# Angles of the trigonometric tables as 16-bit fixed point, and no arithmetic on GpSimd, in a fused linear attention and FFT gate kernel

## The chip, the cores and the metric

The kernel runs on one core of one Trainium2 chip. The core has TensorE (matmuls), VectorE, ScalarE and GpSimd (arithmetic on tiles in on-chip memory) and SyncE (here only for issuing the stores). Each works through its own list of instructions in order and waits for the others by semaphores. The metric is the time of one execution in microseconds of the device. Before the change it is 284.3 us, the median of three runs (283.73 to 285.67).

## What is computed

The reference takes q, k and v (8 batches, 8 heads, 576 positions, 64 features) and does two things in a row. First a linear attention: with `theta = pi/2 * pos / 576`, q and k are passed through relu and doubled into a cosine and a sine half; then

```
kv  = einsum('bhsf,bhsd->bhfd', k_p, v)
num = einsum('bhsf,bhfd->bhsd', q_p, kv)
den = einsum('bhsf,bhf->bhs', q_p, sum(k_p over s))
att = num / (den + 1e-6)
```

The heads are put side by side into x (8 x 576 x 512). Then a gate with a long convolution:

```
x1, x2, x3 = split(x @ w_proj)                     # 512 x 1536
conv = irfft(rfft(x2) * rfft(filter_fft))          # over the 576 positions
out  = (x1 * conv * x3) @ w_out                    # 512 x 512
```

## The kernel before

The 576 positions are held as 96 partitions times 6. A batch goes through these steps, each a function in the code: `emit_phi` (VectorE: relu and the multiplication by cosine, sine or tangent columns, giving the tiles `qp` and `kp`; for q one relu over everything and six multiplications by `tcol`), `emit_va` (ScalarE copies v), `emit_kv` (TensorE), `emit_qt` (TensorE transposes `qp`, VectorE and ScalarE each copy half of the result into `qpt`), `emit_num` (TensorE, then VectorE divides: tile `att`), `emit_fx` (TensorE, a first small transform that also sorts positions; ScalarE copies to `fx`), `emit_x2` (TensorE: the x2 part of the projection, tile `x2f`), `emit_dft` (TensorE with the tables `tre` and `tim`, then VectorE multiplies by the filter's transform `h3`), `emit_gate` (TensorE: x1 and x3, 64 matmuls of 128x288 per batch in four column blocks; ScalarE copies x1 to `x1s`, VectorE multiplies it with x3 into `g`), `emit_inv` (TensorE with the tables `ire` and `iim`), `emit_out` (TensorE, ScalarE, store).

All matmul results go through one ring of four PSUM units (`unit`, line 62), shared by all steps. A step that asks for a fifth unit waits until the first one of the ring has been read. In `emit_gate` every column block takes two units, one that `x1s` frees and one that `g` frees.

The inputs are loaded by GpSimd's queue, with a conversion from 4 to 2 bytes an element, into a ring of four `raw` tiles. Batch 2's q, k and v and all later ones have to wait until an older tile has been read.

The tables are made by the kernel itself at its start, between the steps of batches 0 and 1. There are three sets, each a sine and a cosine table: the forward table (`tre`, `tim`, 96x288, `emit_fwd_tables`), the filter's table (`hs_`, `hc`, 96x864, `emit_h_tables`) and the inverse table (`ire`, `iim`, 96x864, `emit_inv_turns` and `emit_inv_tables`). Each is made in the same way. Index tiles from GpSimd (`fr_i`, `sr_i`, integers) times a factor give the angle in turns, as a float (`tn_fwd`, `tn_h`, `tn_inv`). [...] `sin_cos` (line 288) then has ScalarE take the sine, the absolute value, and a sine shifted by a quarter turn for the cosine (lines 290 to 292).

`emit_h` transforms the filter. The two halves of the filter (`filt16`, 96x1536 each) are added and subtracted into `feo`, on GpSimd (line 421), and TensorE multiplies them with the filter's tables. One row of the inverse table is made apart (`t0`, `t1`, lines 381 to 388).

The order on each engine comes from a scheduler, which takes the instructions by the order of the calls at the end of the program and by its own estimate of when each is ready. `behind(...)` holds an instruction back until a named earlier one has been issued: `feo` is held behind the second GpSimd operation of the inverse angles (the mark "turns"). The calls at the start run from batch 0's attention through `emit_rows`, `emit_inv_turns`, the four blocks of `emit_gate(0, c)`, `emit_fwd_tables`, `emit_x2(0)`, `emit_phi(1, "q")`, `emit_qt(1, .)`, `emit_h_tables`, `emit_phi(1, "k")`, `emit_kv(1)`, `emit_h`, `emit_num(1, .)` and `emit_dft(0)` to `emit_inv_tables` and batch 2. From batch 1 on a loop repeats the same steps without any tables.

Of the kernel before, what the change touches and what calls it, by code (L numbers as in the profile page):

```python
# [13 lines left out]
I32 = mybir.dt.int32  # L14
# [3 lines left out]
def kernel(  # L18
# [51 lines left out]
    half_pi = consts.tile([128, 1], FP32, tag="half_pi", name="half_pi")  # L70
    wr_col = consts.tile([128, 1], FP32, tag="wr_col", name="wr_col")
# [17 lines left out]
    def tsc(out, in0, s1, op0, s2=None, op1=None):  # L89
        if op1 is None:  # L90
            nc.vector.tensor_scalar(out=out, in0=in0, scalar1=s1, scalar2=None, op0=op0)
        else:
            nc.vector.tensor_scalar(out=out, in0=in0, scalar1=s1, scalar2=s2, op0=op0, op1=op1)  # L93
# [178 lines left out]
    def turns_off(nr, turns, ncol, pool=False):  # L272

        a_ = setupp.tile([NP, NCOL], FP32, tag="tg_a", bufs=2, name="tg_a")
        a = a_[0:nr, 0:ncol]
        if pool:
            nc.gpsimd.tensor_scalar(
                out=a, in0=turns, scalar1=RC, scalar2=-RC, op0=AL.add, op1=AL.add
            )
            mark["turns", 0] = nc.gpsimd.tensor_tensor(out=a, in0=a, in1=turns, op=AL.subtract)  # L280
        else:
            nc.vector.tensor_scalar(out=a, in0=turns, scalar1=RC, scalar2=None, op0=AL.add)
            nc.vector.scalar_tensor_tensor(
                out=a, in0=a, scalar=-RC, in1=turns, op0=AL.add, op1=AL.subtract
            )
        return a

    def sin_cos(nr, a, sin_dst, cos_dst):

        nc.scalar.activation(out=sin_dst, in_=a, func=AF.Sin, scale=TWO_PI)  # L290
# [5 lines left out]
    def trig(nr, turns, sin_dst, cos_dst, ncol):  # L296
        sin_cos(nr, turns_off(nr, turns, ncol), sin_dst, cos_dst)
# [22 lines left out]
    def emit_fwd_tables():  # L320
# [18 lines left out]
        tsc(q4, half, 0.25, AL.mult)  # L339
# [5 lines left out]
        trig(NP, tnf, tim.rearrange("p a b -> p (a b)"), tre.rearrange("p a b -> p (a b)"), HS)  # L345
# [17 lines left out]
    def emit_inv_turns():  # L363
        fc = cc["fc"]
        sr_i = cc["sr_i"]
        fcs = small("fcs", 3)
        tsc(fcs, fc, 1.0 / 1152.0, AL.mult)
        tn = setupp.tile([NP, NCOL], FP32, tag="tn_inv", name="tn_inv")
        for bl in range(3):
            nc.scalar.activation(  # L370
                out=tn[:, ds(bl * HS, HS)], in_=sr_i, func=AF.Copy, scale=fcs[0:NP, bl : bl + 1]
            )
        cc["inv_a"] = turns_off(NP, tn, NCOL, True)

    def emit_inv_tables():
        sr_i = cc["sr_i"]
        sin_cos(
            NP, cc["inv_a"], iim.rearrange("p a b -> p (a b)"), ire.rearrange("p a b -> p (a b)")
        )

        t0 = setupp.tile([1, HS], FP32, tag="t0", name="t0")
        tsc(t0, sr_i[0:1], 0.25, AL.mult)
        t1 = setupp.tile([1, HS], FP32, tag="t1", name="t1")
        tsc(t1, t0, RC, AL.add)
        nc.vector.scalar_tensor_tensor(
            out=t1, in0=t1, scalar=-RC, in1=t0, op0=AL.add, op1=AL.subtract
        )
        nc.scalar.activation(out=iim[0:1, 0], in_=t1, func=AF.Sin, scale=TWO_PI)

    def emit_h_tables():  # L390
# [9 lines left out]
        tn = setupp.tile([NP, NCOL], FP32, tag="tn_big", name="tn_h")  # L400
        for j in range(3):
            tsc(tn[:, ds(j * HS, HS)], frf, s3[0:NP, j : j + 1], AL.mult, 1.0 / S, AL.mult)
        trig(NP, tn, hs_.rearrange("p a b -> p (a b)"), hc.rearrange("p a b -> p (a b)"), NCOL)
# [12 lines left out]
    def emit_h():  # L416
        hc, hs_, hb, alt = cc["hc"], cc["hs"], cc["hb"], cc["alt"]
        fa = filt16.rearrange("p x (j n) -> p x j n", j=3)
        for x, op in ((0, AL.add), (1, AL.subtract)):
            with behind("turns", 0):  # L420
                nc.gpsimd.tensor_tensor(
# [31 lines left out]
    def emit_phi(b, nm, h0=0, nh=NH):  # L453
# [11 lines left out]
        for j in range(NJ):  # L465
            for cs, col in ((0, ccol), (1, scol)) if nm == "k" else ((1, tcol),):
                tsc(
# [372 lines left out]
```

## Time and profile before

| | |
|---|---|
| median of three runs | 284.3 us (283.73 to 285.67) |
| the profiled execution | 285.12 us |
| its span on the core | 283.3 us |
| TensorE busy (matmuls) | 250.7 us, 88% |
| VectorE busy | 218.8 us, 77% |
| ScalarE busy | 197.6 us, 70% |
| GpSimd busy | 38.8 us, 14% |
| mean granted TensorE clock | 0.973 of full |

The span is the time from the first to the last instruction on the core; the execution's time is 1.8 us longer. Busy time counts no waiting. In the chain that ended last, followed back from the last store, TensorE has 73% of the span, VectorE 14% and ScalarE 7%. The list of waits puts down each idle stretch of an engine to the instruction that came last before it ended; where several had to come, the named one need not be the one that was late for a reason of its own. The page's strip of 40 slices shows TensorE's share and its granted clock over time: TensorE is at 90% or more in nearly all slices behind the first third, and the granted clock is below 0.9 in three of the slices between 35 and 71 us.

### The profile page before, as it was taken

Reading aid. Unit: us, or ns where it says so; the run is one execution under the profiler, and the core shown is the slowest. Engines: PE = TensorE matmul, PEld = TensorE weight load, DVE = VectorE, ACT = ScalarE, POOL = GpSimd, SP = SyncE. Lnnn points to the kernel's source line nnn. Section 1 sums busy time; section 2 is a strip of 40 time slices with the busy share of each in tenths; the row PEclk is TensorE's granted clock in tenths of the full one; section 3 lists DMA queues with packets and bytes.
Section 4 is the critical chain, followed back from the end, with each engine's and each line's share of the span. In section 5 each row is a group of like instructions: output and inputs, shape, how many; then the busy total and the mean of one; then the engine's idle time right before and its main releaser. Section 6 shows DMA issues by size and latency. Waiting matters only on the chain.

```text
span 283.3 us, 6056 instructions
## 1 busy us (share of the span) xinstructions
PE 250.7 (88%) x2393; PEld 176.5 (62%) x2393; DVE 218.8 (77%) x666; ACT 197.6 (70%) x274; POOL 38.8 (14%) x51
## 2 busy tenths in 40 slices
PE   0387719998899999999999999999999999999991
PEld 0265516755676867686768676867687768755740
DVE  7789999698999768986799579965997269606650
ACT  2366236997948796869676976798679867758252
POOL 8443950130010111011100010010000000000000
PEclk9999957997999999999999999999999999999998
DMA  5999974698624069506960697065000500050405
GB/s 79 184 206 207 204 105 67 86 126 125 86 24 62 8 83 253 78 2 84 240 98 1 87 193 142 0 86 169 1 2 0 147 22 2 0 168 26 126 20 167
DMA packets 26989, 26.67 MB, mean 94 GB/s; under 512 B 1680, under 2 KB 22160, under 8 KB 26960
## 3 DMA queue, kind: packets, MB, share of 16 engines
q0 software_dynamic: 21200, 16.84, 41.3%
q1 hardware_dynamic: 5760, 9.44, 10.8%
q8 instruction: 18, 0.29, 0.4%
q14 instruction: 11, 0.09, 0.1%
HBM read 33.69 MB, written 9.44 MB: 152 GB/s over the span
## 4 chain that ended last, share of the span: by engine, by line
PE 73%; DVE 14%; ACT 7%; DMA 2%; issue 1%; POOL 0%; POOLq 0%
PE x L623 21%; PE x L586 14%; PE out L670 12%; PE inv L649 8%; PE qt L497 5%; DVE qp L93 5%; PE fx L549 4%; PE kv L484 4%; ACT x2f L591 4%; PE num L523 3%; DMA vraw<-in_v_dram 2%; PE dft L600 2%; DVE kp L93 2%; DVE att L533 1%; ACT va L122 1%
## 5 line engine op out<-in xcount | busy, mean ns | idle before, releaser
L623 PE MATMUL x<-fx,wp 128*128 128x288 f16 x512 | 69.9, 292 | 8.5 <-DVE tim L358 7.4
L623 PEld LDWEIGHTS <-wp 128*128 128x128 f16 x512 | 51.0, 100 | 22.3 <-DVE tim L358 7.7
L586 PE MATMUL x<-wp,fx 128*96 128x512 f16 x192 | 44.9, 380 | 0.0
L591 ACT ACTIVATE x2f<-x 96x1024 f16<-96x1024 f32 x24 | 24.5, 1019 | 25.7 <-PE x L586 25.7
L553 ACT CAST fx<-fx 128x960 f16<-128x960 f32 x32 | 30.7, 961 | 15.6 <-PE fx L549 15.6
L670 PE MATMUL out<-wo,y 128*128 128x512 f16 x160 | 37.8, 379 | 0.3
L122 ACT COPY va<-vraw 96x768 f16<-96x768 f16 x32 | 25.6, 846 | 8.9 <-DMA vraw<-in_v_dram 8.9
L586 PEld LDWEIGHTS <-fx 128*96 128x96 f16 x192 | 22.2, 123 | 14.3
L631 DVE TENSOR_TENSOR g<-x,x1s 128x288 f16<-128x288 f32 x64 | 27.2, 449 | 4.3 <-PE x L623 4.3
L533 DVE TENSOR_TENSOR att<-num,rcp 128x640 f16<-128x640 f32 x32 | 26.3, 821 | 0.3
L504 DVE COPY qpt<-qt 128x600 f16<-128x600 f16 x30 | 14.0, 468 | 15.8 <-PE qt L497 15.1
L670 PEld LDWEIGHTS <-y 128*128 128x128 f16 x160 | 15.1, 97 | 16.5 <-DVE y L656 1.2
L602 ACT CAST xf<-dft 96x1024 f16<-96x1024 f32 x24 | 23.5, 1009 | 1.9 <-PE dft L600 1.3
L605 DVE TENSOR_TENSOR m<-xf,h 96x1024 f16<-96x1024 f16 x24 | 16.3, 679 | 10.9 <-ACT xf L602 10.7
L674 ACT ACTIVATE os<-out 128x1024 f32<-128x1024 f32 (+1 forms) x24 | 21.4, 904 | 4.5 <-PE out L670 2.3
L484 PE MATMUL kv<-va,kp 96*128 96x65 f16 x384 | 15.4, 197 | 10.0 <-ACT va L122 8.4
L629 ACT CAST x1s<-x 128x576 f16<-128x576 f32 x32 | 20.4, 639 | 5.5 <-PE x L623 4.7
L497 PEld LDWEIGHTS <-qp 96*128 96x128 f16 x384 | 20.6, 102 | 5.4 <-issue 1.0
L93 DVE TENSOR_SCALAR qp<-qraw,tcol 96x512 f16<-96x512 f16 (+1 forms) x54 | 23.4, 493 | 0.0
L497 PE MATMUL qt<-perm,qp 96*128 96x96 f16 x384 | 22.2, 213 | 0.6 <-ACT fx L553 0.4
L649 PEld LDWEIGHTS <-yf 96*128 96x128 f16 x192 | 18.5, 98 | 5.1 <-DVE yf L609 0.7
L484 PEld LDWEIGHTS <-kp 96*128 96x128 f16 x384 | 14.3, 100 | 11.4 <-DVE kp L93 8.9
(172 smaller groups left out, 400.2 us busy)
## 6 DMA issues: line engine op xcount, KB each, us to landing
out_dram<-os SPq DMA_DIRECT2D x24, 192.0 KB, 2.7
qraw<-in_q_dram POOLq DMA_DIRECT2D x7, 576.0 KB, 7.4
kraw<-in_k_dram POOLq DMA_DIRECT2D x7, 576.0 KB, 7.6
vraw<-in_v_dram POOLq DMA_DIRECT2D x7, 576.0 KB, 6.2
out_dram<-os SPq DMA_DIRECT2D x24, 128.0 KB, 2.5
wp<-in_moe_w_proj_dram POOLq DMA_DIRECT2D x3, 512.0 KB, 11.9
out_dram<-os SPq DMA_DIRECT2D x24, 64.0 KB, 2.4
kraw<-in_k_dram POOLq DMA_DIRECT2D x2, 288.0 KB, 6.2
```

The source lines that it names most:

```text
L93: nc.vector.tensor_scalar(out=out, in0=in0, scalar1=s1, scalar2=s2, op0=op0, op1=op1)
L122: nc.scalar.copy(out=va_buf[b % 2][:, hs, :, 0:D], in_=raw_t[(b, "v")][:, hs].rearrange("p h (j d) -> p h j d", j=NJ),)
L484: nc.tensor.matmul(u[:, h // 4, ds((h % 4) * 65, 65)], kp[:, j, h].rearrange("p a b -> p (a b)"), va[:, h, j, 0:65], start=(j == 0), stop= ...
L497: nc.tensor.transpose(u[:, hh, ds(j * NP, NP)], qp[:, j, 2 * hp + hh].rearrange("p a b -> p (a b)"), perm,)
L533: mark["att", b, hp] = nc.vector.tensor_tensor(out=att[:, :, ds(hp * 128, 128)].rearrange("p t (h d) -> p h t d", h=2), in0=nv[:, :, :, 0: ...
L553: nc.scalar.copy(out=fx[:, c, :, 0:40].rearrange("p g (u o) -> p u g o", u=2), in_=u[:, :, 0:480].rearrange("p u (g o) -> p u g o", o=20),)
L586: nc.tensor.matmul(u[0:NP, comp], fx[:, c, ds(comp * 6 + 2 * bl, 2)].rearrange("p a b -> p (a b)"), wp16[:, c, ds(DM, DM)], start=(c == 0) ...
L591: mark["x2f", b, bl] = nc.scalar.mul(out=x2f[:, bl], in_=u[0:NP], mul=X2SC)
L623: nc.tensor.matmul(u[:, hf, 0:HS], wp16[:, i, ds(w * DM + c * 128, 128)], fx[:, i, ds(12 + 6 * hf, 6)].rearrange("p a b -> p (a b)"), star ...
L631: mark["g", b, c] = nc.vector.tensor_tensor(out=(g[:, c, 0:HS] if hf == 0 else g[:, c, HS:S][:, ::-1]).rearrange("p (j i o) -> p j i o", j ...
L649: nc.tensor.matmul(u[:, comp, 0:HS], yf[:, bl, comp, ds(c * 128, 128)], tab[:, bl], start=(bl == 0), stop=(bl == 2),)
L670: nc.tensor.matmul(u[:, x], y[:, c, ds(OT[t], 128)], wo16[:, c], start=(c == 0), stop=(c == NC - 1),)
```

## The change

The angles are no longer floats in turns but integers with 65536 units to a turn. The multiplication that makes them writes an integer tile (`tn_fwd`, `tn_h`, `tn_inv`, `t0` are now I32, and the factors carry `FX = 65536`), and one bitwise "and" with 65535 in place (`frac`) takes the angle modulo one turn, on VectorE for all tables. `sin_cos` reads the integers directly: the scale 2 pi / 65536 and a bias of minus pi turn the angle half a turn back, which gives minus its sine as before; the absolute value and the shift for the cosine are taken with biases too. Three small constant columns hold the biases. `tg_a` has one buffer instead of two and holds only the absolute value.

The inverse angles' two operations on GpSimd are replaced by one "and" on VectorE, now called in `emit_inv_tables`. The sum and difference `feo` move from GpSimd to VectorE, held behind the last operation of `emit_phi(1, "k")`. GpSimd keeps index fills and the issuing of loads. The one separate row goes from three VectorE operations to two, and is now made in `emit_inv_turns`. All other calls stand where they stood.

```diff
+    m_half_pi = consts.tile([128, 1], FP32, tag="m_half_pi", name="m_half_pi")
+    m_pi = consts.tile([128, 1], FP32, tag="m_pi", name="m_pi")
+    m_half = consts.tile([128, 1], FP32, tag="m_half", name="m_half")
...
+        nc.vector.memset(m_half_pi, -PI / 2.0)
+        nc.vector.memset(m_pi, -PI)
+        nc.vector.memset(m_half, -FX / 2.0)
...
-    def turns_off(nr, turns, ncol, pool=False):
-        a_ = setupp.tile([NP, NCOL], FP32, tag="tg_a", bufs=2, name="tg_a")
-        a = a_[0:nr, 0:ncol]
-        if pool:
-            nc.gpsimd.tensor_scalar(
-                out=a, in0=turns, scalar1=RC, scalar2=-RC, op0=AL.add, op1=AL.add
-            )
-            mark["turns", 0] = nc.gpsimd.tensor_tensor(out=a, in0=a, in1=turns, op=AL.subtract)
-        else:
-            nc.vector.tensor_scalar(out=a, in0=turns, scalar1=RC, scalar2=None, op0=AL.add)
-            nc.vector.scalar_tensor_tensor(
-                out=a, in0=a, scalar=-RC, in1=turns, op0=AL.add, op1=AL.subtract
-            )
-        return a
+    FX = 65536.0
+    def frac(a):
+        nc.vector.tensor_scalar(
+            out=a, in0=a, scalar1=int(FX) - 1, scalar2=None, op0=AL.bitwise_and
+        )
-    def sin_cos(nr, a, sin_dst, cos_dst):
-        nc.scalar.activation(out=sin_dst, in_=a, func=AF.Sin, scale=TWO_PI)
-        nc.scalar.activation(out=a, in_=a, func=AF.Abs)
+    def sin_cos(nr, m, ncol, sin_dst, cos_dst):
+        a_ = setupp.tile([NP, NCOL], FP32, tag="tg_a", bufs=1, name="tg_a")
+        a = a_[0:nr, 0:ncol]
+        nc.scalar.activation(out=sin_dst, in_=m, func=AF.Sin, scale=TWO_PI / FX, bias=m_pi[0:nr])
+        nc.scalar.activation(out=a, in_=m, func=AF.Abs, bias=m_half[0:nr])
         nc.scalar.activation(
-            out=cos_dst, in_=a, func=AF.Sin, scale=-TWO_PI, bias=half_pi[0:nr]
-        )
+            out=cos_dst, in_=a, func=AF.Sin, scale=TWO_PI / FX, bias=m_half_pi[0:nr]
+        )
...
-        tn = setupp.tile([NP, 3, NP], FP32, tag="tn_big", name="tn_fwd")
-        tsc(tn, frow, w[0:NP], AL.mult, 1.0 / 1152.0, AL.mult)
+        tn = setupp.tile([NP, 3, NP], I32, tag="tn_big", name="tn_fwd")
+        tsc(tn, frow, w[0:NP], AL.mult, FX / 1152.0, AL.mult)
...
-        trig(NP, tnf, tim.rearrange("p a b -> p (a b)"), tre.rearrange("p a b -> p (a b)"), HS)
+        frac(tnf)
+        sin_cos(NP, tnf, HS, tim.rearrange("p a b -> p (a b)"), tre.rearrange("p a b -> p (a b)"))
...
-        tn = setupp.tile([NP, NCOL], FP32, tag="tn_inv", name="tn_inv")
+        tn = cc["tn_inv"] = setupp.tile([NP, NCOL], I32, tag="tn_inv", name="tn_inv")
...
-        cc["inv_a"] = turns_off(NP, tn, NCOL, True)
+        t0 = cc["t0"] = setupp.tile([1, HS], I32, tag="t0", name="t0")
+        tsc(t0, sr_i[0:1], FX / 4.0, AL.mult)
+        frac(t0)
 
     def emit_inv_tables():
+        frac(cc["tn_inv"])
         sin_cos(
...
-        tn = setupp.tile([NP, NCOL], FP32, tag="tn_big", name="tn_h")
+        tn = setupp.tile([NP, NCOL], I32, tag="tn_big", name="tn_h")
...
+        frac(tn)
+        sin_cos(NP, tn, NCOL, hs_.rearrange("p a b -> p (a b)"), hc.rearrange("p a b -> p (a b)"))
...
-            with behind("turns", 0):
-                nc.gpsimd.tensor_tensor(
+            with behind("phi", 1, "k"):
+                nc.vector.tensor_tensor(
                     out=feo[:, x].rearrange("p j n -> p (j n)"),
                     in0=filt16[:, 0], in1=filt16[:, 1], op=op,
                 )
```

More of the change, by code (lines that the diff above doesn't have):

```diff
@@ L90, in tsc @@
         if op1 is None:
-            nc.vector.tensor_scalar(out=out, in0=in0, scalar1=s1, scalar2=None, op0=op0)
+            return nc.vector.tensor_scalar(out=out, in0=in0, scalar1=s1, scalar2=None, op0=op0)
         else:
-            nc.vector.tensor_scalar(out=out, in0=in0, scalar1=s1, scalar2=s2, op0=op0, op1=op1)
+            return nc.vector.tensor_scalar(out=out, in0=in0, scalar1=s1, scalar2=s2, op0=op0, op1=op1)
     def rnd(out, in0, mul, add):
@@ L366, in emit_inv_turns @@
         fcs = small("fcs", 3)
-        tsc(fcs, fc, 1.0 / 1152.0, AL.mult)
-        tn = setupp.tile([NP, NCOL], FP32, tag="tn_inv", name="tn_inv")
+        tsc(fcs, fc, FX / 1152.0, AL.mult)
+        tn = cc["tn_inv"] = setupp.tile([NP, NCOL], I32, tag="tn_inv", name="tn_inv")
         for bl in range(3):
@@ L372, in emit_inv_turns @@
             )
-        cc["inv_a"] = turns_off(NP, tn, NCOL, True)
+        t0 = cc["t0"] = setupp.tile([1, HS], I32, tag="t0", name="t0")
+        tsc(t0, sr_i[0:1], FX / 4.0, AL.mult)
+        frac(t0)
     def emit_inv_tables():
-        sr_i = cc["sr_i"]
+        frac(cc["tn_inv"])
         sin_cos(
-            NP, cc["inv_a"], iim.rearrange("p a b -> p (a b)"), ire.rearrange("p a b -> p (a b)")
-        )
[L381 to L386, printed above, removed]
+            NP, cc["tn_inv"], NCOL,
+            iim.rearrange("p a b -> p (a b)"), ire.rearrange("p a b -> p (a b)"),
+        )
+        nc.scalar.activation(
+            out=iim[0:1, 0], in_=cc["t0"], func=AF.Sin, scale=TWO_PI / FX, bias=m_pi[0:1]
         )
-        nc.scalar.activation(out=iim[0:1, 0], in_=t1, func=AF.Sin, scale=TWO_PI)
     def emit_h_tables():
```

9 lines of the change are left out of this document (3 added, 6 removed).

## The prediction

> **What bounds the kernel now.** I read the list of waits first, then TensorE in order of time around the largest stall, then the engines that the stall points to. The page gives TensorE 88% of the span. The table of stretches tells where the rest is (columns: length, busy us and count of PE, PEld, DVE, ACT, POOL, then granted clock, DMA share, GB/s; PE is TensorE, DVE VectorE, ACT ScalarE, POOL GpSimd):
>
> ```profile
> 28.50:33.70 5.20, 5.09 (x41) 3.69 (x38) 5.20 (x4) 1.98 (x3) 5.18 (x4) 1.00 1.22 203
> 33.70:41.10 7.40, 0.01 (x2) 0.01 (x1) 7.33 (x11) 1.21 (x3) 5.54 (x3) 0.64 0.84 132
> 41.10:46.60 5.50, 5.50 (x25) 3.58 (x26) 5.34 (x16) 3.00 (x6) 0.00 (x0) 0.55 0.78 107
> 62.00:75.00 13.00, 10.32 (x117) 7.26 (x116) 12.14 (x30) 11.49 (x16) 0.77 (x1) 0.87 0.89 132
> 100.00:250.00 150.00, 148.79 (x1495) 107.44 (x1494) 116.51 (x327) 117.07 (x159) 6.94 (x9) 1.00 0.41 80
> ```
>
> From 100 us on TensorE is busy 148.79 of 150 us: whatever reaches that stretch earlier ends the kernel earlier, one for one. Before it stands one hole, 33.7 to 41.1 us, and behind the hole a stretch at clock 0.55. TensorE in order of time (start, length, operation, in brackets the idle time before it and its releaser):
>
> ```profile
> 28.48 5.22 PE L623 MATMUL x<-fx,wp 128*128 128x288 f16 x39
> 41.10 5.52 PE L623 MATMUL x<-fx,wp 128*128 128x288 f16 x24 [7.39 <-DVE tim L358]
> 46.45 5.34 PE L586 MATMUL x<-wp,fx 128*96 128x512 f16 x24
> ```
>
> These are the gate matmuls of batch 0, 64 in all, eight to each PSUM unit. The ring has four units, so after five of the eight TensorE needs the unit that VectorE's first gate product (g, L631) reads. The releaser "tim L358" is only what VectorE ran next. Why g was late, VectorE tells:
>
> ```profile
> 28.59 0.98 DVE L93 TENSOR_SCALAR qp<-qraw,tcol 96x512 f16<-96x512 f16 x1
> 29.50 2.93 DVE L93 TENSOR_SCALAR qp<-qraw,tcol 96x512 f16<-96x512 f16 x1
> 32.34 3.17 DVE L93 TENSOR_SCALAR qp<-qraw,tcol 96x512 f16<-96x512 f16 x1
> 35.43 3.16 DVE L93 TENSOR_SCALAR qp<-qraw,tcol 96x512 f16<-96x512 f16 x1
> 38.78 0.34 DVE L93 TENSOR_SCALAR qp<-qraw,tcol 96x512 f16<-96x512 f16 x1
> 40.24 0.80 DVE L631 TENSOR_TENSOR g<-x,x1s 128x288 f16<-128x288 f32 x2
> 55.51 1.66 DVE L93 TENSOR_SCALAR qp<-qraw,tcol 96x512 f16<-96x512 f16 x6
> ```
>
> The same instruction takes 0.34 us or 3 us. For batch 2 all six take 1.66 us; for batch 1 they take from 28.59 to 39.12 us. GpSimd meanwhile:
>
> ```profile
> 25.62 3.81 POOL L277 TENSOR_SCALAR tg_a<-tn_inv 96x864 f32<-96x864 f32 x1 [6.71 <-ACT tn_inv L370]
> 29.39 0.82 POOL L115 DMA_DIRECT2D qraw<-in_q_dram  x1
> 30.24 2.02 POOL L280 TENSOR_TENSOR tg_a<-tg_a,tn_inv 96x864 f32<-96x864 f32 x1
> 32.21 6.24 POOL L421 TENSOR_TENSOR feo<-filt 96x1536 f16<-96x1536 f16 x2
> ```
>
> GpSimd's arithmetic ends at 29.43, 32.26, about 35.4 and 38.45 us; the first four multiplies end at 29.57, 32.43, 35.51 and 38.59, each 0.1 to 0.2 us behind one of those ends. So one multiply of VectorE gets through between two operations of GpSimd. The hole in TensorE is VectorE held up by exactly the three GpSimd lines that the change takes away.
>
> **The change part by part.** *The hole, 7.4 us.* With GpSimd doing no arithmetic, the multiplies start at 28.6 and take 1.66 us, to 30.2. Two tn_h rows follow (0.64 us as a pair), then g: 0.80 us, so 31.7. TensorE asks for that unit at 33.7, 2 us later. What is late next is ScalarE: its Sin of the h table now waits for the new "and" over 864 columns, and the copy x1s of the third gate block stands behind it. The nearest rows for the "and", which this trace doesn't show, and those of its neighbours, in the groups by line (the last figures are count, busy us and mean ns, then idle time) and in order of time:
>
> ```profile
> L283 DVE SCALAR_TENSOR_TENSOR tg_a<-tg_a,tn_h 96x864 f32<-96x864 f32 x1 | 1.0, 1042 | 0.0
> L282 DVE TENSOR_SCALAR tg_a<-tn_h 96x864 f32<-96x864 f32 x1 | 0.6, 593 | 0.0
> L605 DVE TENSOR_TENSOR m<-xf,h 96x1024 f16<-96x1024 f16 x24 | 16.3, 679 | 10.9 <-ACT xf L602 10.7
> L533 DVE TENSOR_TENSOR att<-num,rcp 128x640 f16<-128x640 f32 x32 | 26.3, 821 | 0.3
> 41.32 0.64 DVE L93 TENSOR_SCALAR tn_h<-fr_i,s 96x288 f32<-96x288 int32 x2
> 44.76 0.92 ACT L290 ACTIVATE hs__724<-tg_a 96x864 f16<-96x864 f32 x1 [2.50 <-DVE tg_a L283]
> 45.59 0.62 ACT L629 CAST x1s<-x 128x576 f16<-128x576 f32 x1
> ```
>
> The "and" lies between 0.59 us (one operand, 4-byte elements) and 1.04. The tn_h rows, with integer input, are on the slow side (0.64 us for 2 x 288), so I take 0.9. From g at 31.7: third tn_h and two tiny ones 0.5, "and" 0.9, Sin 0.92, x1s 0.62: 34.7 us. That unit is wanted when all 64 gate matmuls are through, 24 more at 0.13 us behind 33.7, some 0.5 us earlier by the third part below: 36.3. So the hole closes wholly: 7.4, bounds 6.4 (1 us lost on these copies) and 7.4.
>
> *The cold clock, 2.2 us.* Behind the hole 24 matmuls start over 41.10 to 46.45, 0.223 us each, at clock 0.55; the 39 ahead of it took 5.22, 0.134 each. 24 x 0.089 = 2.1; against the last batch,
>
> ```profile
> 260.29 8.00 PE L623 MATMUL x<-fx,wp 128*128 128x288 f16 x64
> ```
>
> 0.125 each, it is 2.35. I take 2.2. No low clock without a hole ahead of it is in the table of stretches.
>
> A rule would make this smaller: the Trainium skill, "TensorE: Matmul & The Clock Gate", Part 1, has the array back at full rate after some 3.4 us of steady work, half of which, an estimate of 1.7 us, would be lost here; by that the time is 0.5 us higher. The trace differs: 0.55 was granted over 5.5 us.
>
> *Order in front of the hole, 0.5 us.* The change turns the forward angles into bounded integers in one step, so their tables are ready before the multiplies. Before, on VectorE (att is the attention output, rcp its divisor, t the angles of one row, qp the multiplies):
>
> ```order
> L385 SCALAR_TENSOR_TENSOR t_952<-t_952,t_950 1x288
> L532 RECIPROCAL rcp_3_446<-rcp_3_446 128x10
> L533 TENSOR_TENSOR att_288<-num_3_434,rcp_3_446 128x2x5x64
> L91 TENSOR_SCALAR qp_651<-qraw_118 96x48x64
> L93 TENSOR_SCALAR qp_651<-qraw_118,tcol 96x8x64 x6
> L282 TENSOR_SCALAR tg_a<-tn_fwd 96x288
> L283 SCALAR_TENSOR_TENSOR tg_a<-tg_a,tn_fwd 96x288
> ```
>
> The forward angles (L282, L283) stand behind the multiplies. At the same place of VectorE's list after the change, with the changed kernel's line numbers (L282 is the "and", L530 the att of L533, tim the sine table):
>
> ```order
> L282 TENSOR_SCALAR tn_fwd<-tn_fwd 96x288
> L529 RECIPROCAL rcp_2_436<-rcp_2_436 128x10
> L526 TENSOR_TENSOR rcp_3_452<-num_3_440,epsc 128x10
> L530 TENSOR_TENSOR att_294<-num_2_424,rcp_2_436 128x2x5x64
> L529 RECIPROCAL rcp_3_452<-rcp_3_452 128x10
> L96 TENSOR_SCALAR jp<-jp 128x1
> L94 TENSOR_SCALAR tim<-tim,amp 96x192
> L530 TENSOR_TENSOR att_294<-num_3_440,rcp_3_452 128x2x5x64
> ```
>
> The angles moved ahead of both att. The row t (L385) no longer stands ahead of the last one, but tim does, which waits for ScalarE's Sin:
>
> ```profile
> 26.98 0.82 DVE L533 TENSOR_TENSOR att<-num,rcp 128x640 f16<-128x640 f32 x1
> 24.56 0.97 ACT L370 ACTIVATE tn_inv<-sr_i,fcs 96x288 f32<-96x288 int32 x2
> 26.86 0.96 ACT L553 CAST fx<-fx 128x960 f16<-128x960 f32 x1 [1.33 <-PE fx L549]
> 39.86 0.44 ACT L290 ACTIVATE tim<-tg_a 96x288 f16<-96x288 f32 x1 [8.54 <-DVE tg_a L283]
> ```
>
> ScalarE is free at 25.5, so the Sin ends at about 26.0 and tim doesn't hold: the last att starts near 26.4 instead of 26.98. The three table activations fit into ScalarE's 1.33 us of idle time (0.44 + 0.44 + 0.53 less overlaps) before the cast at 26.86. 0.5 us, bounds 0 and 0.6 (nothing of att's start gained, or all).
>
> *What VectorE gets, 0 us.* feo (sum and difference, 96x1536, twice) and the "and" of the inverse angles now stand between the last kp and the qpt copies:
>
> ```order
> L96 TENSOR_SCALAR kp_745<-kraw_123,ccol 96x8x64
> L96 TENSOR_SCALAR kp_745<-kraw_123,scol 96x8x64
> L418 TENSOR_TENSOR feo<-filt_86 96x1536 x2
> L282 TENSOR_SCALAR tn_inv<-tn_inv 96x864
> L501 COPY qpt_88<-qt_0_664 128x10x60
> ```
>
> Before, the copies followed the last kp directly, and VectorE stood idle there for 2.08 us. The first row below is that idle time; the others are VectorE's busy time between the multiplies and the last kp, whole and then for the tiles tim, tre and tg_a alone (length, busy us and count):
>
> ```profile
> 52.34 1.49 DVE L504 COPY qpt<-qt 128x600 f16<-128x600 f16 x3 [2.08 <-PE qt L497]
> 39.00:50.30 11.30, 10.91 (x35) 0.69 0.41 56
> 39.05:50.30 11.25, 0.00 (x0) 0.00 (x0) 0.43 (x3) 0.44 (x1) 0.69 0.41 56
> 39.05:50.30 11.25, 0.00 (x0) 0.00 (x0) 0.37 (x2) 0.53 (x1) 0.69 0.41 56
> 39.05:50.30 11.25, 2.38 (x4) 4.28 (x6) 0.00 (x0) 0.69 0.41 56
> ```
>
> By L605 (0.679 us for 1024 half-size elements, two operands) one feo takes 1.02 us; if it ran like L533 (0.821 for 640) it would be 1.97. I take the nearer row, with the same types: 2.0 + 0.9 for the "and" = 2.9 us, bounds 2.6 and 5.0. Of the 10.9 us between multiplies and last kp go the five operations on tim and tre, now done before the multiplies (0.43 + 0.37), and the four on tg_a (2.38), against one "and" (0.9): 8.6 is left. VectorE is at 30.2 + 8.6 + 2.9 = 41.7 us when it comes to the copies. They can start where TensorE's transposes land: x2 from 46.45 - 10.1 = 36.3 (the sum below), 5.2 us for it as before, 0.7 more as before: 42.2. Hidden, by 0.5 us; at the upper bound it costs 1.6. Small edits (three memsets, two operations on one row instead of three) vanish in VectorE's early idle time.
>
> Sum: 7.4 + 2.2 + 0.5 = 10.1 us. The profiled execution took 285.12 us (span 283.3, 1.8 around it), so 275.0 for such a one; it lay 0.8 above the median of the three runs, 284.3, so **274.2**.
>
> **Rivals.** *VectorE bounds the table stage.* All slow bounds together: 1.6 behind feo, 1.0 on the gate copies, no 0.5 in front: gain 7.0, 277.3 us. For it: VectorE is 97% busy in the 5.5 us behind the hole. Against it: the slack above, 0.5 us at the copies, 1.6 at x1s and 2.0 at g. *The clock stays low*, as it also is at 62 to 75 us (0.87): gain 7.9, 276.4. Against it: there too TensorE idles 2.7 of 13 us, so low clock goes with idleness. *Loads come late.* The second batch's k was issued when the multiplies ended:
>
> ```profile
> 39.42 0.79 POOL L115 DMA_DIRECT2D kraw<-in_k_dram  x1 [0.97 <-DVE tg_a L282]
> 57.08 0.55 DVE L93 TENSOR_SCALAR kp<-kraw,ccol 96x512 f16<-96x512 f16 x1
> DMA to landing us min/median/max: 11.1/11.1/11.1
> DMA to landing us min/median/max: 17.6/17.6/17.6
> ```
>
> (The two landings are those of batch 2's q, issued at 29.39, and batch 1's v, the longest.) The issue moves to 30.3; even with 17.6 us to landing k is there at 47.9, against 57.08 - 10.1 = 47.0 when it is first used: 0.9 us late, 275.1.
>
> The Trainium skill speaks against the change here: "SBUF — State Buffer", Who interferes with whom, says that vector operations in a two-port mode and GpSimd exclude each other, so multiplies that run back to back could keep GpSimd from writing descriptors. No such stretching shows in the issues of this trace (0.79 us).
>
> *Slower:* GpSimd is not the cause; the transfers are, which moved 203 GB/s while the multiplies crawled. Then the hole stays, and VectorE gets up to 5.0 us of work where it had 2.08 us of idle time: 2.9 us longer, 287.2. It decides if the multiplies still take over 1 us each. Against it: the ends above, and the last multiplies, 0.34 us each as soon as GpSimd had finished, while transfers went on (132 GB/s over 33.7 to 41.1).
>
> That the change does not do what it says is excluded by the order. GpSimd's list behind its first transfers, before:
>
> ```order
> L146 DMA wo_81<-in_moe_w_out_dram 128x4x512
> L277 TENSOR_SCALAR tg_a<-tn_inv 96x864
> L115 DMA qraw_956<-in_q_dram 96x8x384
> L280 TENSOR_TENSOR tg_a<-tg_a,tn_inv 96x864
> L421 TENSOR_TENSOR feo<-filt_83 96x1536 x2
> L115 DMA kraw_958<-in_k_dram 96x8x384
> ```
>
> The load of batch 2's q and that of its k stand between and behind the arithmetic. After the change the same stretch is:
>
> ```order
> L118 DMA vraw_127<-in_v_dram 96x8x384
> L149 DMA wo_84<-in_moe_w_out_dram 128x4x512
> L118 DMA qraw_957<-in_q_dram 96x8x384
> L118 DMA kraw_959<-in_k_dram 96x8x384
> L118 DMA vraw_961<-in_v_dram 96x8x384
> ```
>
> Only loads are left, each held by its buffer alone; q can go out before 29.4 us, behind wo in the same queue.
>
> **How the numbers follow.** Forecast 0.72, VectorE bound 0.17, clock 0.05, loads 0.03, slower 0.03. The forecast's own range: up by 0.4 (0.6 instead of 0.5, 2.35 instead of 2.2, rounding) and by another 1.3 if the 2.7 us of idle time at 62 to 75 shrink too, since VectorE arrives there with less behind it: 272.5. Upwards the first rival and a further 1.2 for the same idle time growing: 278.5. Over 1% (2.8 us, about what a measurement of this kernel tells from no change) is cleared by every case but the last, which at the cheap end of feo (no loss) would be no change: faster 0.95, same 0.03, slower 0.02.
>
> **What would show it.** Right: six multiplies of batch 1 in about 1.7 us, no stall of TensorE above 1 us between 28 and 45 us, clock 1.00 there, x2 (L586 before) starting near 36.3 instead of 46.45, feo at about 1.0 us each on VectorE, the wait of qpt for TensorE below 1 us. Wrong: multiplies still at 3 us, or TensorE waiting for x1s or qpt by more than 2 us, or the shift of 10 us given back between 50 and 80 us.

## The result and the profile after

| | before | after |
|---|---|---|
| median | 284.01 us (283.40 to 285.67, 4 runs) | 274.09 us (273.69 to 274.49, 4 runs) |
| ratio | | 0.9642, 95% interval 0.9597 to 0.9686 |
| the profiled execution | 285.12 us | 273.88 us |
| its span | 283.3 us | 272.0 us |
| mean granted TensorE clock | 0.973 | 0.988 |

The four runs of before are the three named ahead of the prediction and one more. The change makes the kernel 9.9 us faster by the medians. Between the two profiled executions lie 11.2 us; the one of before was slower than its median by 1.1 us, the one of after faster by 0.2 us. The steps below are counted between the profiled executions, since only these have rows.

The table of stretches of the kernel after (columns as in the prediction: length, busy us and count of PE, PEld, DVE, ACT, POOL, then granted clock, DMA share, GB/s):

```profile
27.00:35.00 8.00, 8.00 (x67) 6.29 (x65) 8.00 (x29) 5.88 (x9) 0.77 (x1) 1.00 1.22 208
35.00:45.00 10.00, 9.32 (x124) 6.84 (x123) 8.82 (x23) 8.84 (x13) 0.94 (x2) 1.00 1.22 186
51.00:64.00 13.00, 10.27 (x119) 7.55 (x119) 12.77 (x32) 11.90 (x16) 1.04 (x2) 0.87 0.88 130
90.00:240.00 150.00, 148.79 (x1493) 107.52 (x1492) 115.14 (x323) 116.58 (x158) 6.93 (x9) 1.00 0.40 80
```

Where before had its hole, TensorE is now busy in 8.00 of 8 us and then in 9.32 of 10, at full clock. The long stretch behind is as full as it was (148.79 of 150 us), so what arrives there earlier ends earlier. TensorE of the kernel after in order of time, from the gate matmuls on (L620, before L623), then x2 (L583), the transposes (L494) and the first stall behind them:

```profile
27.19 8.16 PE L620 MATMUL x<-fx,wp 128*128 128x288 f16 x64
35.18 5.34 PE L583 MATMUL x<-wp,fx 128*96 128x512 f16 x24
40.36 2.50 PE L494 MATMUL qt<-perm,qp 96*128 96x96 f16 x48
44.59 0.54 PE L481 MATMUL kv<-va,kp 96*128 96x65 f16 x12 [0.54 <-ACT va L125]
52.01 0.77 PE L520 MATMUL num<-kvs,qpt 128*128 128x65 f16 x20 [0.22 <-DVE h L94]
```

All 64 gate matmuls are one group of 8.16 us without idle time ahead of any of them; before they were 39, a hole of 7.39, and 24 at a low clock. x2 starts at 35.18 instead of 46.45. VectorE of the kernel after, the rows that answer to the prediction's:

```profile
24.30 0.30 DVE L282 TENSOR_SCALAR tn_fwd<-tn_fwd 96x288 int32<-96x288 int32 x1
25.81 0.81 DVE L530 TENSOR_TENSOR att<-num,rcp 128x640 f16<-128x640 f32 x1
28.02 1.66 DVE L96 TENSOR_SCALAR qp<-qraw,tcol 96x512 f16<-96x512 f16 x6
30.16 0.81 DVE L628 TENSOR_TENSOR g<-x,x1s 128x288 f16<-128x288 f32 x2
38.14 1.82 DVE L418 TENSOR_TENSOR feo<-filt 96x1536 f16<-96x1536 f16 x2
39.88 0.60 DVE L282 TENSOR_SCALAR tn_inv<-tn_inv 96x864 int32<-96x864 int32 x1
41.08 1.49 DVE L501 COPY qpt<-qt 128x600 f16<-128x600 f16 x3 [0.60 <-PE qt L494]
```

The six multiplies take 1.66 us while the transfers move 208 GB/s. The first g starts at 30.16; before it came in a pair at 40.24. Both additions are there (feo 1.82 us for two, the "and" 0.60), and VectorE still waits 0.60 us for TensorE at the copies. GpSimd has nothing but loads in this part of its list:

```profile
21.06 0.90 POOL L118 DMA_DIRECT2D qraw<-in_q_dram  x1 [1.61 <-DVE fc L312]
29.98 0.77 POOL L118 DMA_DIRECT2D kraw<-in_k_dram  x1 [8.01 <-DVE qp L96]
```

Batch 2's q goes out at 21.06 instead of 29.39 us, its k at 29.98 instead of 39.42.

### The profile page after: what moved, and what is told of

Same layout as the page of the kernel before. It is cut to its first block, busy times and chain, and to the rows that moved or that the text cites. A ratio compares the mean times of both kernels' runs of the same rounds, so it can differ in the third digit from the quotient of the medians.

```text
span 272.0 us, 6054 instructions
## 1 busy us (share of the span) xinstructions
PE 247.0 (91%) x2393; PEld 175.1 (64%) x2393; DVE 209.5 (77%) x669; ACT 198.2 (73%) x274; POOL 27.1 (10%) x47
## 4 chain that ended last, share of the span: by engine, by line
PE 77%; DVE 9%; ACT 8%; DMA 2%; issue 1%; POOL 0%; POOLq 0%
PE x L620 23%; PE x L583 14%; PE out L667 12%; PE inv L646 8%; PE qt L494 5%; PE fx L546 4%; PE kv L481 4%; ACT x2f L588 4%; PE num L520 3%; DMA vraw<-in_v_dram 2%; PE dft L597 2%; DVE kp L96 2%; ACT va L125 2%; DVE att L530 1%; DVE qp L96 1%; ACT xf L599 1%
## 5 line engine op out<-in xcount | busy, mean ns | idle before, releaser
L620 PE MATMUL x<-fx,wp 128*128 128x288 f16 x512 | 67.1, 286 | 0.0
L620 PEld LDWEIGHTS <-wp 128*128 128x128 f16 x512 | 50.0, 98 | 13.2 <-issue 0.2
L583 PE MATMUL x<-wp,fx 128*96 128x512 f16 x192 | 44.9, 380 | 0.0
L583 PEld LDWEIGHTS <-fx 128*96 128x96 f16 x192 | 22.2, 123 | 14.3
L494 PEld LDWEIGHTS <-qp 96*128 96x128 f16 x384 | 20.5, 102 | 5.4 <-issue 1.1
L494 PE MATMUL qt<-perm,qp 96*128 96x96 f16 x384 | 22.2, 213 | 0.5 <-ACT fx L550 0.3
L546 PE MATMUL fx<-fm,att 128*128 128x240 f16 x128 | 18.8, 270 | 2.6 <-DVE att L530 1.2
```

Of the source, the lines that this page charges most:

```text
L494: nc.tensor.transpose(u[:, hh, ds(j * NP, NP)], qp[:, j, 2 * hp + hh].rearrange("p a b -> p (a b)"), perm,)
L546: nc.tensor.matmul(u[:, t // 2, 0:480].rearrange("p (g o) -> p g o", o=20)[:, :, ds((t % 2) * 10, 10)], att[:, t, ds(c * 128, 128)], fm, s ...
L583: nc.tensor.matmul(u[0:NP, comp], fx[:, c, ds(comp * 6 + 2 * bl, 2)].rearrange("p a b -> p (a b)"), wp16[:, c, ds(DM, DM)], start=(c == 0) ...
L620: nc.tensor.matmul(u[:, hf, 0:HS], wp16[:, i, ds(w * DM + c * 128, 128)], fx[:, i, ds(12 + 6 * hf, 6)].rearrange("p a b -> p (a b)"), star ...
```

## The experiments

The theory: an operation of GpSimd holds one operation of VectorE until it ends, the hole of TensorE is the sum of these holds, and the 16-bit angles matter only since they take the work off GpSimd. The rivals: the transfers stretch the multiplies; the cheaper angles or the new order of the list bring the time; only arithmetic that reads memory holds VectorE. Every ratio below is against the kernel before in runs on the same chip.

**One move alone: feo.** The kernel before, in which only the sum and difference go to VectorE. Angles stay floats, and GpSimd still rounds the inverse ones and takes the whole turns off, in two operations (L277 and L280).

```diff
-            with behind("turns", 0):
-                nc.gpsimd.tensor_tensor(
+            with behind("phi", 1, "k"):
+                nc.vector.tensor_tensor(
```

> The kernel before with one part of the change: sum and difference feo on VectorE, angles as before (floats, the inverse ones rounded on GpSimd). Theory 1 (a GpSimd operation with tile operands holds up VectorE's multiplies): GpSimd works until about 32.3 us, so two of the six multiplies are held to 29.6 and 32.4 us and four run in 0.26 us each, to 33.5; then the forward angles stand ahead of g, so g ends near 35.6 and TensorE idles about 1.9 us instead of 7.4. Too short to cool the clock fully: gain 5.5 to 7.5, time 276.5 to 278.5. Theory 2 (transfers or something else stretch the multiplies): all six still take about 10 us, time 284 to 287.

Measured: 279.65 us (278.54 to 281.69), ratio 0.9839 (0.978 to 0.9899). This is 1.1 us above the range that was expected. GpSimd and VectorE of this kernel, in order of time:

```profile
25.00 3.80 POOL L277 TENSOR_SCALAR tg_a<-tn_inv 96x864 f32<-96x864 f32 x1 [6.35 <-ACT tn_inv L370]
29.62 2.02 POOL L280 TENSOR_TENSOR tg_a<-tg_a,tn_inv 96x864 f32<-96x864 f32 x1
```

```profile
27.97 4.88 DVE L93 TENSOR_SCALAR qp<-qraw,tcol 96x512 f16<-96x512 f16 x6
```

and its TensorE:

```profile
34.83 3.12 PE L623 MATMUL x<-fx,wp 128*128 128x288 f16 x24 [1.74 <-DVE tim L358]
46.78 0.67 PE L497 MATMUL qt<-perm,qp 96*128 96x96 f16 x12 [1.70 <-ACT x2f L591]
```

Two GpSimd operations remain and stretch the six multiplies from 1.66 to 4.88 us; the hole shrinks from 7.39 to 1.74 us. What was not expected is the second stall. The tables come later here, ScalarE makes the last x2f copy late, and TensorE waits 1.70 us for it; behind that the clock is low for 6.8 us (48.0 to 54.8). At the start of x2 this kernel was 8.1 us ahead of before (37.78 against 46.45 us, less 0.6 us by which this execution ran ahead from its start on), at the end of the span only 4.7: it lost 3.4 us behind x2, where this stall and this low clock lie.

**The other move alone: the inverse angles.** The kernel before, in which the inverse angles are rounded on VectorE in `emit_inv_tables`, as floats, and feo stays on GpSimd.

```diff
-        cc["inv_a"] = turns_off(NP, tn, NCOL, True)
+        cc["tn_inv"] = tn
...
     def emit_inv_tables():
+        cc["inv_a"] = turns_off(NP, cc["tn_inv"], NCOL)
```

> The kernel before with the other part alone: the inverse angles rounded on VectorE (floats), feo still on GpSimd, where it now waits only for the filter's load (about 32 us). Theory 1: the six multiplies of batch 1 run before that, in 1.7 us, but from 32 to 38.5 us GpSimd's two feo operations hold whichever fast VectorE operation comes next, one each 3 us (a kp multiplication or hb), so g of the third or fourth gate block is late and TensorE idles some 2 to 4 us near 36 us with a cool clock behind: time 276 to 280. Theory 2: multiplies unchanged at about 10 us, time 284 to 286.

Measured: 277.88 us (276.84 to 279.42), ratio 0.9787 (0.973 to 0.9844), as expected. GpSimd, then VectorE of this kernel:

```profile
31.13 6.95 POOL L422 TENSOR_TENSOR feo<-filt 96x1536 f16<-96x1536 f16 x2 [12.65 <-DMA filt<-in_moe_filter_fft_dram]
```

```profile
27.92 1.13 DVE L93 TENSOR_SCALAR qp<-qraw,tcol 96x512 f16<-96x512 f16 x4
31.18 0.81 DVE L632 TENSOR_TENSOR g<-x,x1s 128x288 f16<-128x288 f32 x2
31.91 3.22 DVE L283 SCALAR_TENSOR_TENSOR tg_a<-tg_a,tn_h 96x864 f32<-96x864 f32 x1
35.05 3.18 DVE L93 TENSOR_SCALAR kp<-kraw,ccol 96x512 f16<-96x512 f16 x1
38.15 0.81 DVE L632 TENSOR_TENSOR g<-x,x1s 128x288 f16<-128x288 f32 x2
```

GpSimd is idle until 31.13, and the multiplies are free. Then it has two operations up to 38.08 us, and exactly two operations of VectorE are stretched, whatever they are: L283 from 1.04 to 3.22 us and one multiply of k from 0.34 to 3.18. The hold goes with GpSimd's operations in time, not with the line of the program. The two g at 31.18, each with one operand in PSUM, ran beside the first feo and were not stretched (0.81 us). TensorE runs the 64 gate matmuls without a break and stalls once, further back, in x2:

```profile
39.01 5.34 PE L587 MATMUL x<-wp,fx 128*96 128x512 f16 x16 [2.50 <-DVE g L632]
```

Alone the two moves bring 4.9 and 6.6 us against the 284.52 us that before took beside them.

**Both moves, float angles.** The two edits above together: the change without its 16-bit format.

> Both moves off GpSimd, but the angles stay floats in turns with two rounding operations on VectorE each: tells what the 16-bit format alone brings. VectorE gets some 0.5 us more in front of the last att, 1.0 ahead of g and about 2.3 more (second operation over 864 columns, three small rows) between the last kp and the qpt copies, where the changed kernel has 0.6 us of slack. If the gain is the emptied GpSimd: 275 to 276.5, one to two us behind the changed kernel. If the format is what counts: 280 or more.

Measured: 273.83 us (273.13 to 273.99), ratio 0.9622 (0.958 to 0.9664): the whole gain, and 1.2 us better than the range expected for it. The fixed-point format brings nothing measurable of its own. VectorE of this kernel at the place where the floats cost more:

```profile
38.97 1.82 DVE L422 TENSOR_TENSOR feo<-filt 96x1536 f16<-96x1536 f16 x2
40.71 0.60 DVE L282 TENSOR_SCALAR tg_a<-tn_inv 96x864 f32<-96x864 f32 x1
41.45 1.04 DVE L283 SCALAR_TENSOR_TENSOR tg_a<-tg_a,tn_inv 96x864 f32<-96x864 f32 x1
42.41 1.58 DVE L505 COPY qpt<-qt 128x600 f16<-128x600 f16 x4
```

The copies start at 42.41 without waiting, 1.3 us later than after the change (41.08). I had counted that lateness as lost. Nearly all of it is not. The kv matmuls start 0.9 us later (43.61 against 42.75), but after the change their last part waits 0.54 us for ScalarE's va, and here they run without a break: the first filter matmuls start at 45.13 us here and at 44.97 after the change.

**The work put back on GpSimd, without use.** The kernel after, and GpSimd runs the four operations of before into a scratch tile that nothing reads; the load of batch 2's k stands behind them in its list, as before.

```diff
+        scr = setupp.tile([NP, NCOL], FP32, tag="scr", name="scr")
+        nc.gpsimd.tensor_scalar(
+            out=scr, in0=tn, scalar1=RC, scalar2=-RC, op0=AL.add, op1=AL.add
+        )
+        mark["turns", 0] = nc.gpsimd.tensor_tensor(out=scr, in0=scr, in1=scr, op=AL.subtract)
+        for x, op in ((0, AL.add), (1, AL.subtract)):
+            with behind("turns", 0):
+                mark["scr", 1] = nc.gpsimd.tensor_tensor(
+                    out=scr.bitcast(FP16)[:, 0 : 3 * DM], in0=filt16[:, 0], in1=filt16[:, 1], op=op
+                )
```

> The changed kernel, with the four GpSimd operations of before put back at their place but written into a scratch tile that nobody reads: nothing depends on them, the results are unchanged. Theory 1: VectorE's multiplies end near 38.5 us again, TensorE idles some 7 us, the clock falls: 282 to 285. Theory 2 (the GpSimd results were late, or the order of the work was the cause): 274 to 275, since nobody waits for the scratch tile.

Measured: 282.24 us (281.63 to 283.75), ratio 0.9937 (0.9904 to 0.997), as expected. VectorE, then TensorE of this kernel:

```profile
28.89 10.11 DVE L96 TENSOR_SCALAR qp<-qraw,tcol 96x512 f16<-96x512 f16 x6
```

```profile
40.34 4.38 PE L631 MATMUL x<-fx,wp 128*128 128x288 f16 x24 [7.07 <-DVE g L639]
```

Nobody waits for these operations, all else but the place of two loads (batch 2's q goes out at 29.57 us, its k at 39.30) is as in the kernel after, and the hole is back (7.07 us against 7.39), with 10.11 us for the six multiplies. So the hole comes from GpSimd being busy beside VectorE, not from a result that comes late and not from the list's order. Of the 2.3 us that this kernel keeps against before, 2.0 are in the rows: the order in front of the hole (0.6), 0.3 of the hole, and a shorter low clock behind it (4.38 us for the 24 matmuls against 5.52).

**Write-only work on GpSimd.** The kernel after, and GpSimd fills the scratch tile ten times with an index. A fill's row names no tile that it reads. A copy of one column on ScalarE times the first.

```diff
+        scr = setupp.tile([NP, NCOL], I32, tag="scr", name="scr")
+        nc.scalar.copy(out=scr[:, 0:1], in_=tn[:, 0:1])
+        for x in range(10):
+            mark["scr", 1] = nc.gpsimd.iota(scr, pattern=[[1, NCOL]], base=x, channel_multiplier=0)
```

> The changed kernel, with ten index fills of 96x864 on GpSimd (they write a scratch tile that nobody uses, and read no tile) in place of the four thrown-away operations, from about 25.5 us on; a fill of 96x288 took 0.40 us before, so each should take about 1 us. Theory A: any GpSimd operation on tiles holds VectorE's fast operations: each of the six multiplies waits for a fill, they take 4 to 6 us instead of 1.7, the first g ends near 34 to 36 us, TensorE idles 1 to 3 us: 275.5 to 279. Theory B: only GpSimd operations that read tiles hold VectorE: multiplies 1.7 us, time 274 to 275.

Measured: 279.42 us (278.62 to 280.53), ratio 0.983 (0.9793 to 0.9867), close above the range of the first theory and far from the second's. GpSimd, VectorE and TensorE of this kernel:

```profile
27.45 8.83 POOL L375 IOTA scr<- 96x864 int32 x9
```

```profile
30.07 5.43 DVE L96 TENSOR_SCALAR qp<-qraw,tcol 96x512 f16<-96x512 f16 x6
```

```profile
37.50 4.79 PE L625 MATMUL x<-fx,wp 128*128 128x288 f16 x24 [4.36 <-DVE g L633]
```

The nine fills follow each other every 0.98 us, the six multiplies every 0.90: one multiply for each fill. The hold lasts about as long as GpSimd's own operation, here 0.9 us, there 3 us. Holding needs no reading. TensorE idles longer than the 1 to 3 us expected, since the fills held VectorE ahead of the multiplies too: the relu over the same q took 1.53 us instead of 0.95.

**A try for more: k later.** The kernel after, with the twelve multiplies of batch 2's k moved from 45.9 us to behind the last att of batch 1.

```diff
         emit_phi(2, "q")
-        emit_phi(2, "k")
+    with behind("att", 1, 3):
+        emit_phi(2, "k")
```

> The changed kernel, with the twelve kp multiplications of batch 2 issued behind batch 1's last att instead of ahead of it (3.1 us of VectorE's work moved back), an attempt at a faster version: after the change TensorE still idles 2.3 us between 51 and 59 us, where VectorE is busy without a break, and the clock is 0.67 from 59 to 64 us. If VectorE's place in that chain is the bound: the att come up to 1.5 us earlier, gain 1 to 2 us, 272 to 273. If ScalarE (busy without a break from 55 on) or the later use of kp bounds: within 0.5 us of the changed kernel, or up to 1 us slower since kv of batch 2 then waits.

Measured: 278.52 us (278.25 to 279.48), ratio 0.9803 (0.9773 to 0.9832): 4.4 us slower than after, where a small gain was hoped for. VectorE, then TensorE of this kernel:

```profile
64.08 1.59 DVE L501 COPY qpt<-qt 128x600 f16<-128x600 f16 x4
```

```profile
61.93 0.80 PE L560 MATMUL fxc<-fm,att 128*128 128x192 f16 x4 [1.05 <-ACT fx L550]
63.62 1.12 PE L494 MATMUL qt<-perm,qp 96*128 96x96 f16 x12 [0.89 <-ACT fx L564]
65.28 0.88 PE L646 MATMUL inv<-ire,yf 96*128 96x288 f16 x3 [0.55 <-ACT qpt L505]
```

The scheduler put VectorE's copies of batch 2's transposed q (qpt) behind the multiplies: all four run from 64.08 us, instead of at 57.19, 58.35, 60.72 and 63.29. Until a copy has run, its unit of the PSUM ring stays taken. My reading was that three of the four units are held in this way from 59.5 us on, so that the matmuls and ScalarE's copies alternate through the one unit left, and that the idle time then brings a low clock (0.50 from 60.8 to 71.1 us). The rival: VectorE, busy in 12.77 of 13 us there, has no room for 3.1 us more.

**k later, but behind the copies.** As the last, but the multiplies stand behind the last of the four copies.

```diff
-        emit_phi(2, "k")
...
+    with behind("qpt", 2, 3):
+        emit_phi(2, "k")
```

> The twelve multiplies of batch 2's k now stand behind VectorE's last copy of batch 2's transposed q, not ahead of these copies as in the kernel before this one. Theory R (the copies hold units of the PSUM ring, and TensorE stalls when they come late): the four copies run one by one between 57 and 64 us again, no stall of TensorE over 1.1 us between 59 and 66, one low-clock stretch of 3.4 us there and not three, time 273 to 275 us. Rival V (VectorE simply has no room for 3.1 us of work behind 51 us, wherever it stands): the delay moves to the point where the k is first used (kv of batch 2), TensorE stalls there by 2 us or more, time 276.5 us or more.

Measured: 273.33 us (272.41 to 273.52), ratio 0.9604 (0.9562 to 0.9645). TensorE of this kernel:

```profile
57.99 0.57 PE L546 MATMUL fx<-fm,att 128*128 128x240 f16 x4 [0.97 <-ACT xf L599]
59.41 0.57 PE L546 MATMUL fx<-fm,att 128*128 128x240 f16 x4 [0.19 <-ACT fx L550]
60.82 0.67 PE L494 MATMUL qt<-perm,qp 96*128 96x96 f16 x12 [0.37 <-ACT fx L550]
```

The same 3.1 us of VectorE work, later still, and the stalls of 1.05, 0.89 and 0.55 us are gone; no low clock shows until TensorE has done its last matmul. That is not the chance of one profile: the mean granted clock is 0.993 to 0.996 in all four runs of this kernel and 0.988 to 0.991 in the four of after. So it was the copies and the ring, not the lack of room. This is the fastest kernel of the study by its median, 0.8 us below after; the two ratios' intervals overlap, so that it beats the change is likely but not shown.

**Both kernels once more, unedited.** In the profiles of the kernels up to k later, every stretch of low clock (read off the table of stretches in steps of 0.1 us) is a multiple of 3.41 us long. These two runs, one execution each, ask whether the stretches have their own beat.

> The changed kernel once more, unedited. Theory G (the clock is set in stretches of 3.41 us that run by themselves, whatever the kernel does): low stretches are again a whole number of 3.41 us long; where they lie against the kernel may differ by up to 3.4 us from 60.6 to 64.1, or there may be none or two. Rival (the kernel's own stall sets the start of the low clock): it starts again within 0.3 us of 60.6. Time 273.5 to 274.7 us.

> The kernel before once more, unedited. Theory G: the hole of 7.4 us is there, the low clock in and behind it lasts two or three times 3.41 us, and the 24 matmuls behind the hole take between 4.3 and 5.6 us according to where the stretches lie. Rival: 5.5 us again, within 0.1. Time 283 to 286 us, low when the 24 matmuls are quick.

Measured: 274.04 us and 284.61 us. The low clock in all nine kernels, behind 24 us. Each profile also ends at low clock, from 2.1 to 5.0 us behind TensorE's last matmul on; the record cuts that stretch off, and it is left out here and below:

| kernel | low from, to (us) | length | TensorE busy in the 3.41 us ahead |
|---|---|---|---|
| before | 35.8 to 46.1; 66.5 to 70.0 | 10.24; 3.41 | 1.26; 2.07 |
| before again | 35.3 to 45.6; 66.0 to 69.5 | 10.24; 3.41 | 1.27; 2.04 |
| after | 60.6 to 64.1 | 3.41 | 1.95 |
| after again | 55.5 to 59.0 | 3.41 | 2.19 |
| feo only | 48.0 to 54.8 | 6.83 | 1.71 |
| angles only | 40.2 to 43.7 | 3.41 | 1.24 |
| both, float | 54.9 to 58.3 | 3.41 | 1.97 |
| work put back | 36.1 to 43.0 | 6.83 | 0.53 |
| index fills | 38.4 to 41.9 | 3.41 | 0.95 |
| k later | 60.8 to 71.1 | 10.24 | 1.97 |
| k behind the copies | none | | |

The kernel after has its low stretch 5.1 us earlier the second time, though its gate matmuls start only 0.45 us later (27.64 against 27.19): the stall does not set the start alone. For before the second run does not tell the two theories apart, since the stretches fell at the same place within its own 0.5 us earlier start, and its 24 matmuls took 5.53 us again.

## Why the prediction was right, step by step

*The hole, 7.4 us:* right in mechanism and size. Restoring GpSimd's work alone restores the hole (7.07 us), and removing either move's half of it leaves a smaller stall (1.74 and 2.50 us). That the transfers stretch the multiplies is refuted: 1.66 us for six at 208 GB/s.

*The cold clock, 2.2 us:* the rows give 2.35: 24 matmuls took 5.35 us to the start of x2 before, and now take 3.0 of the 7.99 us for 64. The matmuls in front of the hole, which I had left out, gained 0.2 us: 39 took 5.23 us to its start, and now 40 take 5.0. The two rates that I weighed against each other, one stretch of 3.4 us against the 5.5 us seen, were no contradiction. In the kernel before, cut at the beat:

```profile
35.85:39.26 3.41, 0.00 (x0) 0.00 (x0) 3.41 (x4) 0.00 (x0) 2.60 (x1) 0.50 0.96 148
39.26:42.68 3.42, 1.58 (x7) 1.04 (x8) 3.35 (x13) 2.37 (x5) 0.79 (x1) 0.50 0.51 53
42.68:46.09 3.41, 3.41 (x17) 2.12 (x15) 3.41 (x10) 1.33 (x2) 0.00 (x0) 0.51 0.82 128
46.09:49.50 3.41, 3.41 (x19) 2.06 (x18) 3.12 (x12) 3.08 (x5) 0.00 (x0) 1.00 0.01 2
```

The hole ended at 41.10, in the middle of a stretch. That stretch and the next, the first in which TensorE worked throughout, stayed low: 1.6 + 3.4 = 5.0 us at half clock. The Trainium skill, "TensorE: Matmul & The Clock Gate", Part 1, says that the clock is judged over a window of about 3.4 us that runs by itself, and that the number of slow matmuls therefore depends on where the work falls in it; these rows and the table above agree. The size of this term was to that extent luck: after a hole of nearly the same length the "work put back" kernel had 24 matmuls in 4.38 us. The profiled execution of before was also one with more low clock than most: the runs of before at a mean granted clock of 0.973, it among them, took 284.6 to 285.9 us, those at 0.977 to 0.985 took 283.05 to 285.2.

*Order in front of the hole, 0.5 us:* measured 0.55, from the num matmuls of batch 0's third pair of heads to the steady gate matmuls: 24.17 to 28.48 us before, 23.43 to 27.19 after. The size was right, the cause only in part. The prediction saw rightly that the forward angles move ahead of both att and the row t away from between them, but it put this down to the integers made in one step. It does not come from the format of the angles: with floats and both moves the two att stand 1.06 us apart as after (1.05), and with the inverse angles alone moved, in floats, 1.05 too (24.20 and 25.25); there as well the forward angles stand ahead of both att and t does not stand between them. With feo alone moved it is 1.61 as before (1.60). So this gain comes with taking the inverse angles off GpSimd.

*What VectorE gets, 0 us:* right, and with more room. The "and" took 0.60, not 0.9: it runs like the one-operand float row L282 (0.59), not like the slower rows with integer input. Two feo took 1.82, not 2.0. The slack at the copies was 0.60 us where 0.5 was forecast, since TensorE also came 0.4 us sooner. Even with no slack, as with float angles, 1.3 us of lateness at the copies left 0.2 at the filter matmuls, because kv otherwise waited for ScalarE. So the upper bound, 1.6 us lost here, was an overestimate as far as the first 1.3 us of lateness go.

*The sum.* x2 starts 11.27 us earlier. Of that 0.74 us lie ahead of everything the change touches (the same early cast of sgn stands at 21.43 and 20.69 us; two executions of one kernel differ there by up to 0.5 us), 0.55 are the order, 7.39 the hole, 2.35 the cold clock, 0.24 the first gate matmuls and rounding. Without the 0.74 the shift is 10.5, against 10.1 forecast; at the second half of num it is 63.50 to 52.01, that is 10.75, and at the end of the span (283.3 to 272.0) 10.6. Nothing was given back on the way. The medians differ by 9.9, since the profiled run of before lay above its median by more than I had subtracted (1.1 us by four runs, not 0.8).

*The rivals.* VectorE as the bound did not come: it is busy in 8.82 of the 10 us behind 35 us, and waits. The clock is low once behind the stage, as before, for 3.41 us. The k of batch 2 was issued at 29.98 and its first multiply ran at 45.93 without waiting. The slower case is out with the transfers. The rule by which multiplies that run back to back could hold up GpSimd's issues, for which I saw no sign, did show, in two experiments, with 4.27 us where the inverse angles alone were moved and here: GpSimd and VectorE of the kernel with both moves and floats,

```profile
47.32 3.23 POOL L115 DMA_DIRECT2D kraw<-in_k_dram  x1 [3.33 <-DVE qp L93]
50.54 0.77 POOL L115 DMA_DIRECT2D vraw<-in_v_dram  x1
```

```profile
46.95 0.33 DVE L93 TENSOR_SCALAR kp<-kraw,ccol 96x512 f16<-96x512 f16 x1
49.84 0.34 DVE L93 TENSOR_SCALAR kp<-kraw,scol 96x512 f16<-96x512 f16 x1
```

An issue that takes 0.77 us alone takes 3.23, until just after the last of the twelve multiplies (50.18). So the hold works in both directions, and either engine can be the one that waits: after the change the issues took 0.77 to 0.90 us, and at the one that fell among the twelve multiplies (46.30 us) it was a multiply that took 0.54 us instead of 0.34. The long issue cost nothing measurable, since that kernel ran in 273.83 us.

My own misses came in the experiments: feo alone (a second stall behind ScalarE), both moves with floats (a cost that was hidden), the index fills (a stall longer than expected), and k later (a queue position that held PSUM units).

## What to carry to other kernels

A VectorE instruction that takes 3 us here and 0.34 us there is worth setting against GpSimd's rows in time: if each long one ends with a GpSimd operation, price that operation by the VectorE queue behind it, and try it as a dummy that nobody reads before rewriting any arithmetic. Moving work to a busier engine cost nothing here, since the next engine waited for something else anyway, and moving it back in the list cost 4.4 us when copies that free PSUM units ended up behind it. Count low clock in stretches of its own beat, not in proportion to the stall: a stall too short to spoil a stretch brought none (1.74 us with feo alone), and one that spoiled it brought at least 3.41 us at half clock.

## What the runs showed of the hardware that was not expected

- Low clock ahead of TensorE's last matmul came in 3.41, 6.83 or 10.24 us, never another length, in twelve stretches of eleven profiles. The 3.41 us ahead of a fall had TensorE busy in 0.53 to 2.19 us. The limit is not sharp in this measure: one stretch with 1.52 us busy (index fills) brought no fall, and stretches with 2.09 and 2.12 brought none while one with 2.19 did. In two kernels a stretch that was 2.87 (k later) and 3.41 us busy (feo only) was still followed by a low one. What exactly the clock counts stays open.
- GpSimd's index fills, which read nothing, hold the multiplies of VectorE as its arithmetic does, for about the length of one fill (0.90 us for a multiply, a fill every 0.98). The Trainium skill, "SBUF — State Buffer", Who interferes with whom, has it that a VectorE operation in a two-port mode and GpSimd shut each other out for a whole instruction; these times agree, though no row names a mode.
- An operation with two operands in SBUF was held too (L283, 3.22 us instead of 1.04), but the gate product, with one operand in PSUM, was not (0.81 us beside feo).
- No cost of the integer input shows on ScalarE. Its Sin over 96x864 took 0.92 us before and 1.01 after, but it now reads a column as bias too (`m_pi`). The kernel before already had an activation of the same size with such a column, and with a float input it took 1.01 us as well; before, then after:

```profile
47.06 1.01 ACT L292 ACTIVATE hc<-tg_a,half_pi 96x864 f16<-96x864 f32 x1
```

```profile
31.92 1.01 ACT L290 ACTIVATE hs__729<-tn_h,m_pi 96x864 f16<-96x864 int32 x1 [0.80 <-DVE tn_h L282]
```

So the 0.09 us go with the column. TensorE waited for none of these activations.
